# Bias loads before a memset, wide warm matmuls, early first requests and a shorter instruction stream in a gated recurrent-attention and MLP kernel

## The chip, the cores and the metric

The kernel runs on one core of a Trainium2 chip. The metric is the device time of one execution in microseconds (us), lower is better. Beside the time of each run there is one profiled execution, from which all rows below come. The engines are PE (TensorE, with its weight loads shown as PEld), DVE (VectorE), ACT (ScalarE), POOL (GpSimd) and SP (SyncE, which here only issues transfers).

## The reference

```python
g = sigmoid((x * gate_w).sum(-1))                     # x: 2048 x 512
# A: 64 segments of 32 rows, one after the other, with a memory of 8 rows
for s in range(64):
    h = concat([mem, x_s])                            # 40 rows
    q, k, v = h @ Wq, h @ Wk, h @ Wv                  # 32 heads of 128
    p = softmax(mask(q @ k.T * 128 ** -0.5))          # memory keys seen by all, the others causal
    o = (p @ v) @ Wo
    mem, out_s = o[:8], o[8:]                         # the next segment needs mem
# B: per row
y = gelu(layernorm(x) @ w1 + b1) @ w2 + b2            # inner width 1376
out = g * a + (1 - g) * y
```

All arrays are bfloat16. Part A is a chain: the memory that a segment leaves is an input of the next.

## The kernel before

The program is unrolled and the order of the instructions of each engine is written out by hand (`tc.manual_schedule()`). It has a start, a phase for part B, and 64 steps for part A.

**The start.** POOL makes the identity (`ident`, by `make_identity`), sets the last rows of `w2_sb` to zero (line 91), clears the bias tile `b1r` (line 92) and loads the bias into it by two transfers of its own queue (lines 93 and 94). SP and ACT issue the loads of `x` and of the first weights: `w1_sb` in three pieces (columns 0 to 383, then 384 to 895 by line 336, then the rest by line 337), `w2_sb` in pieces too. PE runs `NWARM = 28` matmuls of the identity on itself (line 520), 128 columns each, whose result nobody reads; then it transposes the first two normalized tiles (`prep_tr`, line 447), then the bias (line 525), and then begins part B.

**Part B.** The 16 tiles of 128 rows go in eight blocks of two. For each of 11 columns of the inner width, `a_mm` (line 468) multiplies by `w1` and ACT applies gelu with the bias; `b_mm` (line 475) follows two units later and multiplies by `w2`. Tiles in `DEF = (1, 3, 5, 7, 11, 13)` skip `b_mm` there: `spill` writes their gelu output to DRAM (`h_dr`, line 489), and the second matmul is done later, in the steps. `prep_tr` for the next block begins at unit 8 of a block whose odd tile is deferred, else at unit 6 (line 547). The weights of part A are loaded during this phase.

**The steps.** Step `s` handles segment `s`; four steps (`si` 0 to 3) make a tile. A step's PE work, in order: 64 matmuls for q and k of the 32 rows (line 127, reading `hT`), scores of half the heads (265, 269), v (146), sums of the exponentials (681, 276, 279), the other scores, the rest of v, the values (289, 294), then `wo_pass` (line 158), then `new_mem`, which transposes the new memory rows by matmuls (line 724) in three pieces, each copied by DVE into the next `hT` (line 726). The next step's q and k wait for these copies. DVE's reciprocals go through DRAM (`r_dr`, line 695) and come back broadcast (`Rb`, line 696).

Between these, work that waits for nothing fills PE's pauses. `side(T, si)` gives projections for the next tile, and in the third step of each tile `wo_left`, or for the first tile `mlp_units(8)`. The deferred matmuls come as a generator, `mlp_halves` (line 649): each deferred tile has 11 pieces, and each piece is done in two halves of four matmuls (line 656). Every step takes two halves, by two `next(mlp, None)`; `mlp_units(8)` takes 16 more in step 2. The pieces `hm` are read from DRAM by `hm_load` on SP's queue (line 634), five buffers deep: four are requested when the generator is first advanced, which is within step 0, and then one after each piece. `hm_load4` brings four more at once in step 2. After the last half of a tile, `mlp_out` (line 646) scales the sum on DVE and writes it to `c_dr`; `c_load` reads it back two tiles later.

After the last step an `If` holds a slow path for numerically bad data, which doesn't run here.

Of the kernel before, what the change touches and what calls it, by code (L numbers as in the profile page):

```python
# [27 lines left out]
def kernel(ctx, tc, A_x, A_mem0, A_Wq, A_Wk, A_Wv, A_Wo, A_seg_len, B_x, B_w1, B_b1, B_w2, B_b2, gate_w, out):  # L28
    nc = tc.nc
    P = 128  # L30
    _, S, Dm = A_x.shape
# [9 lines left out]
    FC = (F + P - 1) // P  # L41
# [20 lines left out]
    ident = pers.tile([P, P], BF16)  # L62
    g_all = pers.tile([P, NT], FP32)
    omg = pers.tile([P, NT], FP32)
    w2_sb = pers.tile([P, FC, Dm], BF16)
    c_dr = dram.tile([S, Dm], BF16, name="c_dr")
    DEF = (1, 3, 5, 7, 11, 13)
    h_dr = {T: dram.tile([FC, P, P], BF16, name=f"h_dr{T}") for T in DEF}
    r_dr = [dram.tile([P, NG], FP32, name=f"r_dr{i}") for i in range(2)]

# [17 lines left out]
    b1r = ep.tile([FC, P], BF16)  # L88
    FR = F - (FC - 1) * P
    make_identity(nc, ident[:])  # L90
    nc.gpsimd.memset(w2_sb[FR:P, FC - 1, :], 0.0)
    nc.gpsimd.memset(b1r[:], 0.0)
    nc.gpsimd.dma_start(b1r[0:FC - 1, :], B_b1[0:(FC - 1) * P].rearrange("(c p) -> c p", p=P))
    nc.gpsimd.dma_start(b1r[FC - 1:FC, 0:FR], B_b1[(FC - 1) * P:F].rearrange("(o p) -> o p", o=1))
    nc.gpsimd.memset(BO[:], 0.0)
    for g in range(4):
        nc.gpsimd.memset(BO[32 * g:32 * g + 32, 32 * g:32 * g + 32], 1.0)
# [12 lines left out]
    U = [lps.tile([P, 512], FP32, name=f"U{i}") for i in range(4)]  # L110
    X1 = lps.tile([P, 512], FP32)
# [42 lines left out]
    def wo_group(bk, U_, n):  # L154
        j, ih = HORD[n]
        for c in range(4):
            i = 4 * ih + c
            nc.tensor.matmul(bk[32 * c:32 * c + 32, :], lhsT=U_[:, j, i, :], rhs=Wo_sb[:, 4 * i + j, :],  # L158
                             start=(n == 0), stop=(n == NW - 1), tile_position=(0, 32 * c))
# [13 lines left out]
    def left_qk(T, t, hf, bk):  # L173
        for kc in range(KC):
            qk_unit(bk, gl(T), t, hf, kc)
            if kc < KC - 1:
                yield
        def ca():
            Tb = qk_cast(bk[:])
            dve_q.append(lambda: qk_tr(Tb, QL[T % 2], hf) if t == 0 else kl_tr(Tb, T, hf))  # L180
        act_q.append(ca)
        yield
# [6 lines left out]
    def left_v(T, vb, bk):  # L189
        if vb == 0:  # L190
            VLs[T] = ew.tile([P, 4, 2, Dh], BF16, tag="VL", bufs=1, name="VL")
        for kc in range(KC):
            v_unit(bk, gl(T), vb, kc)
            if kc < KC - 1:
                yield

        def ca():
            VL = VLs[T]
            nc.scalar.copy(out=VL[:, :, vb, :], in_=bk[:].rearrange("p (a e) -> p a e", a=4))

            if vb == 1:
                vp_load(T, 0)
        act_q.append(ca)
        yield
# [8 lines left out]
    def wo_left(T, bk):  # L213
        for n in range(NW):
            wo_group(bk, UL[T % 2], n)
            if n < NW - 1:
                yield

        def ca():
            wl = cw.tile([P, Dm], BF16, tag="wl", name="wl")  # L220
            nc.scalar.copy(out=wl[:], in_=bk[:])
            wls[T] = wl
        act_q.append(ca)
        yield
# [75 lines left out]
    with tc.tile_pool(name="mlpw", bufs=1) as mlpw, \  # L300
# [26 lines left out]
        w1v = B_w1.rearrange("(kc p) f -> p kc f", p=P)  # L327
        nc.sync.dma_start(w1_sb[:, :, 0:F0], w1v[:, :, 0:F0])

        NWARM = 28  # L330
        H1, H2, F1 = 3, 6, 7 * P
        for a, b in ((0, H1), (H1, H2)):
            nc.scalar.dma_start(w2_sb[:, a:b, :], B_w2[a * P:b * P, :].rearrange("(fc p) d -> p fc d", p=P))
# [109 lines left out]
        def prep_tr(blk, tt):  # L443
            y, bk = ys.pop(blk * TB + tt), (X1, X2)[tt]
            tp = bk[:].bitcast(BF16)[:, 0:Dm].rearrange("p (k t) -> p k t", k=KC)
            for kc in range(KC):
                nc.tensor.transpose(tp[:, kc, :], y[:, kc * P:(kc + 1) * P], ident[:])
            nc.vector.tensor_copy(out=yTs[blk][:, :, tt * P:(tt + 1) * P], in_=tp)
# [22 lines left out]
        def b_mm(blk, fc):  # L471
            rows = min(P, F - fc * P + 1)
            tts = [tt for tt in range(TB) if blk * TB + tt not in DEF]
            for tt in tts:
# [9 lines left out]
        def spill(blk, a, b):  # L484
            for tt in range(TB):
                T = blk * TB + tt
                if T in DEF:
                    src = hTm[blk % 2][:, :, tt * P:(tt + 1) * P]
# [27 lines left out]
        dummy = msmall.tile([P, 1], FP32, tag="dummy", name="dummy")  # L516
        nc.scalar.activation(out=dummy[:], in_=ident[:, 0:1], func=ACTF.Sqrt)

        for _ in range(NWARM):
            nc.tensor.matmul(U[3][:, 0:P], lhsT=ident[:], rhs=ident[:], start=True, stop=True, skip_group_check=True)  # L520
        b1p = W[:].bitcast(BF16)[:, 0:FC]
        prep(0)
        for tt in range(TB):
            prep_tr(0, tt)
        nc.tensor.transpose(b1p, b1r[:], ident[:FC, :FC])
        nc.vector.tensor_copy(out=b1_sb[:], in_=b1p)
        side0 = iter(())
# [2 lines left out]
        for n, (blk, fc) in enumerate(units):  # L530
# [15 lines left out]
            if blk + 1 < NBLK:  # L546
                f0 = 8 if (blk + 1) * TB - 1 in DEF else 7 if blk == 0 else 6
                if fc == 7:
# [58 lines left out]
    def chain(*gens):  # L607
        for x in gens:
            yield from x

    def side(T, si):
        gens = []
        if si == 2:
            gens = [wo_left(T - 1, X1) if T >= 1 else mlp_units(8)]
        elif T + 1 < NT:
            gens = [[left_qk(T + 1, 0, 0, X1), left_qk(T + 1, 1, 0, U[3])], [left_qk(T + 1, 0, 1, X1), left_qk(T + 1, 1, 1, U[3])], [],
                    [left_v(T + 1, 0, X1), left_v(T + 1, 1, U[3])]][si]
        return chain(*gens)
# [6 lines left out]

    work = [(T, fc) for T in DEF for fc in range(FC)]
    hms = []

    def hm_load(n):
        for _ in range(n):  # L630
            if work:
                T, fc = work.pop(0)
                hm = cw.tile([P, P], BF16, tag="hm", bufs=5, name="hm")
                nc.sync.dma_start(hm[:], h_dr[T][fc])
                hms.append((T, fc, hm, 1))
# [8 lines left out]
    def mlp_out(T):  # L644
        ct = cw.tile([P, Dm], BF16, tag="o", bufs=1, name="ct")
        nc.vector.tensor_scalar(out=ct[:], in0=W[:], scalar1=omg[:, T:T + 1], scalar2=None, op0=ALU.mult)
        nc.sync.dma_start(c_dr[T * P:(T + 1) * P, :], ct[:])

    def mlp_halves():
        hm_load(4)  # L650
        while hms:
            T, fc, hm, n = hms.pop(0)
            for h in range(2):
                cc = slice(256 * h, 256 * h + 256)
                for c in range(4):
                    nc.tensor.matmul(W[32 * c:32 * c + 32, cc], lhsT=hm[:, 32 * c:32 * c + 32], rhs=w2_sb[:, fc, cc],  # L656
                                     start=(fc == 0 and h == 0), stop=(fc == FC - 1), skip_group_check=True, tile_position=(0, 32 * c))
                if h == 1:
                    hm_load(n)
                    if fc == FC - 1:  # L660
                        mlp_out(T)
                yield

    def mlp_units(n):
        for _ in range(n):
            next(mlp, None)
            next(mlp, None)
            yield

    mlp = mlp_halves()  # L670
    XRs, Rbs = {}, {}

# [57 lines left out]
    for s in range(nseg):  # L730
        T, si = divmod(s, SPT)
        last = s == nseg - 1
        hc, hn = hT[s % 3], hT[(s + 1) % 3]
        W1, W2, W3 = WS[si]
        fill = side(T, si)
        if s + 1 < nseg:
            prep_h(s + 1)
# [134 lines left out]
    for bk, cc in halves:  # L872
        for i in range(SPT):
            nc.tensor.matmul(bk[32 * i:32 * i + 32, cc], lhsT=SelL[:, 32 * i:32 * i + 32], rhs=wl[:, cc], start=True, stop=False,
                             skip_group_check=True, tile_position=(0, 32 * i))
        for i in range(si):
            nc.tensor.matmul(bk[32 * i:32 * i + 32, cc], lhsT=SelR[:], rhs=ws[SPT * T + i][:, cc], start=False, stop=True,
                             skip_group_check=True, tile_position=(0, 32 * i))
# [4 lines left out]
    for bk, cc in halves:  # L883
        nc.tensor.matmul(bk[32 * si:32 * si + 32, cc], lhsT=SelI[:], rhs=wf[:, cc], start=False, stop=True,
                         skip_group_check=True, tile_position=(0, 32 * si))
# [125 lines left out]
```

## Time and profile before

| | before |
|---|---|
| median of 3 runs | 766.25 us (765.21 to 767.55) |
| the profiled execution's own time | 766.38 us |
| its span, first to last instruction | 764.6 us |
| mean granted TensorE clock | 0.997 |
| instructions in the trace | 44,823, of them 19,648 matmuls and as many weight loads |
| busy: PE, ACT, DVE, POOL | 97%, 70%, 52%, 36% of the span |

The profile has several views. The page gives each engine's busy time and the transfers by queue. The chain of waits follows the work that ended last back from the end: its rows have start, duration and what ran, and "issue" is time in which an engine waited for nothing that the profile shows. The view of waits sums, for each pair of waiting instruction and releaser, the total, the count and the longest. The timeline lists instructions in order of time, with the idle time before them in brackets. The view of windows gives, for stretches of time, the busy time and the count of instructions of each engine, then the granted clock, the share of the transfer engines that was busy and GB/s. The DMA view counts transfers and packets that start in a window; queue q8 of kind "instruction" carries instructions of an engine.

### The profile page before, as it was taken

What the parts mean: (1) busy time and instruction counts of PE and PEld (TensorE: products, weight loads), DVE (VectorE), ACT (ScalarE), POOL (GpSimd) and SP (SyncE); (2) the same over time, 40 slices, a digit from 0 to 9 for tenths busy, and PEclk for the clock granted to TensorE, in tenths of its full rate; (3) what the DMA queues carried; (4) which work ended last, traced back from release to release, by engine and by line L of the source; (5) the groups of instructions that cost most, each with busy time, mean ns of one, the idle gap of its engine ahead of it and who ended that gap; (6) DMA issues with size and microseconds to landing.
All of it is one profiled execution on the core that took longest, in us unless ns stands there. A gap on an engine that the chain in (4) does not pass through costs nothing.

```text
span 764.6 us, 44823 instructions
## 1 busy us (share of the span) xinstructions
PE 743.3 (97%) x19648; PEld 428.0 (56%) x19648; DVE 400.1 (52%) x1434; ACT 536.9 (70%) x1625; POOL 275.4 (36%) x517
## 2 busy tenths in 40 slices
PE   7999999999999999999999999999999999999996
PEld 5666455556555555555555655556555555555543
DVE  5877354545445454545455445545454555455444
ACT  4666676777777777777777777777777777777763
POOL 4001142443433444333443433443424443343441
PEclk9999999999999999999999999999999999999999
DMA  7999522213222212223132323222222313222211
GB/s 248 339 328 300 153 76 79 74 43 92 66 92 75 79 51 83 77 80 86 36 92 66 94 66 91 70 60 77 80 79 69 81 52 93 63 84 69 73 62 43
DMA packets 71994, 74.96 MB, mean 98 GB/s; under 512 B 39401, under 2 KB 61906, under 8 KB 70258
## 3 DMA queue, kind: packets, MB, share of 16 engines
q1 hardware_dynamic: 70354, 69.96, 29.5%
q8 instruction: 155, 2.54, 1.4%
q0 software_dynamic: 496, 1.18, 0.4%
q10 hardware_dynamic: 944, 0.92, 0.4%
q14 instruction: 45, 0.37, 0.2%
HBM read 59.13 MB, written 6.62 MB: 86 GB/s over the span
## 4 chain that ended last, share of the span: by engine, by line
PE 93%; DVE 2%; ACT 1%; DMA 1%; issue 1%; POOL 0%; DVEq 0%; POOLq 0%; ACTq 0%
PE U L127 33%; PE X L158 19%; PE X L146 16%; PE X L127 4%; PE U L289 3%; PE U L475 2%; PE SbF L468 2%; PE W L468 2%; PE W L656 2%; PE U L146 2%; PE U L265 1%; PE U L724 1%; PE SbF L265 1%; PE SbF L681 1%; DMA b1r<-in_B_b_dram 1%
## 5 line engine op out<-in xcount | busy, mean ns | idle before, releaser
L708 POOL TENSOR_TENSOR UT<-XR,Rb 128x384 bf16<-128x384 bf16 x126 | 140.3, 1137 | 300.9 <-DMA Rb<-r_dr 246.9
L132 ACT CAST Tb<-U 128x512 bf16<-128x512 f32 x288 | 168.9, 587 | 82.5 <-PE U L127 80.7
L127 PEld LDWEIGHTS <-hT 128*32 128x32 bf16 x4096 | 108.9, 96 | 100.0 <-DVE hT L726 8.7
L146 PE MATMUL X<-Wv_sb,hT 128*32 128x512 bf16 x2048 | 144.6, 378 | 0.6 <-issue 0.6
L127 PE MATMUL U<-Wq_sb,hT 128*32 128x512 bf16 x2048 | 137.0, 381 | 0.6 <-DVE hT L726 0.6
L127 PE MATMUL U<-Wk_sb,hT 128*32 128x512 bf16 x2048 | 133.4, 379 | 0.0
L158 PE MATMUL X<-Wo_sb,UT 128*32 128x512 bf16 x2016 | 122.8, 380 | 2.5 <-issue 1.0
L726 DVE CAST hT<-U 128x8 bf16<-128x8 f32 x126 | 21.0, 167 | 166.6 <-PE U L724 125.5
L786 ACT CAST V<-X 128x256 bf16<-128x256 f32 x256 | 88.7, 372 | 16.9 <-PE X L146 5.0
L136 DVE STREAM_TRANSPOSE QT<-Tb 128x256 f32<-128x256 f32 x128 | 56.6, 442 | 73.7 <-ACT Tb L132 73.5
L158 PEld LDWEIGHTS <-UT 128*32 128x32 bf16 x2080 | 59.5, 96 | 57.6 <-issue 19.4
L687 ACT CAST XR<-U 128x256 bf16<-128x256 f32 x252 | 78.4, 434 | 0.0
L715 ACT CAST w<-X 128x128 bf16<-128x128 f32 x189 | 44.7, 309 | 47.2 <-PE X L158 47.2
L136 DVE STREAM_TRANSPOSE KT<-Tb 128x256 f32<-128x256 f32 x128 | 57.0, 445 | 31.1 <-ACT Tb L132 23.2
L708 POOL TENSOR_TENSOR UL<-XR,Rb 128x128 bf16<-128x128 bf16 x126 | 60.6, 505 | 0.0
L146 PEld LDWEIGHTS <-hT 128*32 128x32 bf16 x2048 | 47.3, 94 | 21.3 <-issue 0.9
L700 POOL TENSOR_TENSOR racc<-racc,R 128x72 f32<-128x72 f32 x63 | 21.3, 338 | 101.8 <-DVE R L698 81.2
L815 ACT CAST UT<-U 128x64 bf16<-128x64 f32 x252 | 35.3, 226 | 22.5 <-PE U L294 22.5
L468 PEld LDWEIGHTS <-w_sb 128*128 128x128 bf16 (+1 forms) x352 | 34.0, 102 | 18.1 <-issue 5.5
L769 ACT ACTIVATE E<-U 128x64 bf16<-128x64 f32 (+1 forms) x128 | 35.0, 273 | 10.9 <-PE U L269 10.7
L724 PEld LDWEIGHTS <-w 128*32 128x32 bf16 x1008 | 23.7, 93 | 31.8 <-ACT w L715 25.1
L127 PE MATMUL X<-Wq_sb,GL 128*32 128x512 bf16 x496 | 39.3, 381 | 0.7 <-issue 0.7
(169 smaller groups left out, 1236.7 us busy)
## 6 DMA issues: line engine op xcount, KB each, us to landing
Rb<-r_dr SPq DMA_DIRECT2D x63, 512.0 KB, 3.8
Wv_sb<-in_A_Wv_dram SPq DMA_DIRECT2D x4, 1024.0 KB, 6.4
Wq_sb<-in_A_Wq_dram SPq DMA_DIRECT2D x4, 1024.0 KB, 7.4
Wk_sb<-in_A_Wk_dram SPq DMA_DIRECT2D x4, 1024.0 KB, 8.8
Wo_sb<-in_A_Wo_dram SPq DMA_DIRECT2D x4, 1024.0 KB, 11.8
VP<-VL SPq DMA_DIRECT2D x64, 64.0 KB, 3.2
c<-c_dr SPq DMA_DIRECT2D x16, 128.0 KB, 3.2
hm<-h_dr SPq DMA_DIRECT2D x62, 32.0 KB, 3.3
```

What stands on the lines that cost most here:

```text
L127: nc.tensor.matmul(bk[32 * j:32 * j + 32, :], lhsT=G[:, kc, :], rhs=W5[t][:, kc, h0:h1, j, :], start=(kc == 0), stop=(kc == KC - 1), tile_ ...
L132: nc.scalar.copy(out=Tb[:], in_=bk.rearrange("p (a b e) -> p a e b", a=8, b=2))
L136: nc.vector.transpose(out=dst[:, 8 * hf:8 * hf + 8, c0:c0 + 32, :].rearrange("p a r b -> p a (r b)").bitcast(FP32), in_=Tb[:].rearrange("p ...
L146: nc.tensor.matmul(bk[32 * j:32 * j + 32, :], lhsT=G[:, kc, :], rhs=Wv5[:, kc, 4 * vb:4 * vb + 4, j, :], start=(kc == 0), stop=(kc == KC - ...
L158: nc.tensor.matmul(bk[32 * c:32 * c + 32, :], lhsT=U_[:, j, i, :], rhs=Wo_sb[:, 4 * i + j, :], start=(n == 0), stop=(n == NW - 1), tile_po ...
L468: nc.tensor.matmul(hp[:rows, 0:TB * P], lhsT=w1_sb[:, kc, fc * P:fc * P + rows], rhs=yTs[blk][:, kc, :], start=(kc == 0), stop=(kc == KC - 1))
L687: nc.scalar.copy(out=XR[:, j], in_=U[j][:, 0:NG * 40].rearrange("p (i q) -> p i q", q=40)[:, :, 0:32])
L708: nc.gpsimd.tensor_tensor(out=out[:, :, 4 * h:4 * h + 4, o:o + b - a], in0=XR[:, :, 4 * h:4 * h + 4, a:b], in1=Rb[:, h, :, :, a:b], op=ALU ...
L715: nc.scalar.copy(out=w[:, a:b], in_=bk[:, a:b])
L769: nc.scalar.activation(out=E[:, 4 * i2:4 * i2 + 4, c], in_=Sb[i2][:, :, c], func=ACTF.Exp, scale=scale)
L786: nc.scalar.copy(out=V[:, i0:i0 + 2, :].rearrange("p i e -> p (i e)"), in_=(X1, X2)[vb][:, 256 * h:256 * h + 256])
L815: nc.scalar.copy(out=UT[s % 2][:, j, :, 0:M], in_=U[j][:, 0:NG * 40].rearrange("p (i q) -> p i q", q=40)[:, :, 32:40])
```

## The change

Six edits:

1. The memset of `w2_sb`'s last rows goes behind the two bias loads on POOL.
2. The 28 warm matmuls of 128 columns become 13 of 512 columns (the identity read four times over), and two more of these stand between the first transposes and that of the bias.
3. `DEF` has tile 9 in place of tile 7.
4. `mlp_units(8)` becomes `mlp_units(7)`.
5. The first four requests of `hm` are made ahead of the steps, right after part B, and no more at the generator's first advance.
6. What follows from 2 and 4: 13 pairs of weight load and matmul and 8 matmuls with their weight loads, 42 instructions, are gone from PE's order ahead of steps 3 to 58; one instruction that only waits has come in within step 0. From step 59 on the 16 instructions of edit 4 have been made up. SP's queue has its first four `hm` requests ahead of the `VP` load and the `xT` load of step 0, where before they were behind them.

```diff
--- before.py
+++ after.py
@@ -64,7 +64,7 @@
     omg = pers.tile([P, NT], FP32)
     w2_sb = pers.tile([P, FC, Dm], BF16)
     c_dr = dram.tile([S, Dm], BF16, name="c_dr")
-    DEF = (1, 3, 5, 7, 11, 13)
+    DEF = (1, 3, 5, 9, 11, 13)
     h_dr = {T: dram.tile([FC, P, P], BF16, name=f"h_dr{T}") for T in DEF}
     r_dr = [dram.tile([P, NG], FP32, name=f"r_dr{i}") for i in range(2)]
 
@@ -88,10 +88,10 @@
     b1r = ep.tile([FC, P], BF16)
     FR = F - (FC - 1) * P
     make_identity(nc, ident[:])
-    nc.gpsimd.memset(w2_sb[FR:P, FC - 1, :], 0.0)
     nc.gpsimd.memset(b1r[:], 0.0)
     nc.gpsimd.dma_start(b1r[0:FC - 1, :], B_b1[0:(FC - 1) * P].rearrange("(c p) -> c p", p=P))
     nc.gpsimd.dma_start(b1r[FC - 1:FC, 0:FR], B_b1[(FC - 1) * P:F].rearrange("(o p) -> o p", o=1))
+    nc.gpsimd.memset(w2_sb[FR:P, FC - 1, :], 0.0)
     nc.gpsimd.memset(BO[:], 0.0)
     for g in range(4):
         nc.gpsimd.memset(BO[32 * g:32 * g + 32, 32 * g:32 * g + 32], 1.0)
@@ -327,7 +327,7 @@
         w1v = B_w1.rearrange("(kc p) f -> p kc f", p=P)
         nc.sync.dma_start(w1_sb[:, :, 0:F0], w1v[:, :, 0:F0])
 
-        NWARM = 28
+        NWARM = 13
         H1, H2, F1 = 3, 6, 7 * P
         for a, b in ((0, H1), (H1, H2)):
             nc.scalar.dma_start(w2_sb[:, a:b, :], B_w2[a * P:b * P, :].rearrange("(fc p) d -> p fc d", p=P))
@@ -516,12 +516,16 @@
         dummy = msmall.tile([P, 1], FP32, tag="dummy", name="dummy")
         nc.scalar.activation(out=dummy[:], in_=ident[:, 0:1], func=ACTF.Sqrt)
 
-        for _ in range(NWARM):
-            nc.tensor.matmul(U[3][:, 0:P], lhsT=ident[:], rhs=ident[:], start=True, stop=True, skip_group_check=True)
+        def warm(n):
+            for _ in range(n):
+                nc.tensor.matmul(U[3][:].rearrange("p (a b) -> p a b", a=4), lhsT=ident[:], rhs=ident[:].unsqueeze(1).to_broadcast([P, 4, P]), start=True, stop=True, skip_group_check=True)
+
+        warm(NWARM)
         b1p = W[:].bitcast(BF16)[:, 0:FC]
         prep(0)
         for tt in range(TB):
             prep_tr(0, tt)
+        warm(2)
         nc.tensor.transpose(b1p, b1r[:], ident[:FC, :FC])
         nc.vector.tensor_copy(out=b1_sb[:], in_=b1p)
         side0 = iter(())
@@ -611,7 +615,7 @@
     def side(T, si):
         gens = []
         if si == 2:
-            gens = [wo_left(T - 1, X1) if T >= 1 else mlp_units(8)]
+            gens = [wo_left(T - 1, X1) if T >= 1 else mlp_units(7)]
         elif T + 1 < NT:
             gens = [[left_qk(T + 1, 0, 0, X1), left_qk(T + 1, 1, 0, U[3])], [left_qk(T + 1, 0, 1, X1), left_qk(T + 1, 1, 1, U[3])], [],
                     [left_v(T + 1, 0, X1), left_v(T + 1, 1, U[3])]][si]
@@ -647,7 +651,6 @@
         nc.sync.dma_start(c_dr[T * P:(T + 1) * P, :], ct[:])
 
     def mlp_halves():
-        hm_load(4)
         while hms:
             T, fc, hm, n = hms.pop(0)
             for h in range(2):
@@ -667,6 +670,7 @@
             next(mlp, None)
             yield
 
+    hm_load(4)
     mlp = mlp_halves()
     XRs, Rbs = {}, {}
 
```

## The prediction

> **What bounds the kernel now.** I read the page first, for which engine carries the time.
>
> ```profile
> PE 743.3 (97%) x19648; PEld 428.0 (56%) x19648; DVE 400.1 (52%) x1434; ACT 536.9 (70%) x1625; POOL 275.4 (36%) x517
> ...
> q8 instruction: 155, 2.54, 1.4%
> ```
>
> TensorE (PE) is busy 97% of the span; every other engine has room. So only two things shorten the kernel: less PE work, or fewer moments in which PE stands or is slowed. The change removes almost no work (13 of 19,648 matmuls), so I looked for the moments. The view of PE's waits names one in the first step (and one at the start, in part 4); the chain of waits, in order of time, gives the beginning of each step (its 64 matmuls of line 127), and with that a quiet measure to hold the others against.
>
> ```profile
> PE W L656 <- DMA hm<-h_dr: 1.2, 1, 1.2
> ```
>
> ```profile
> 109.55 3.55 PE U L127 x64
> ...
> 131.51 3.55 PE U L127 x64
> ...
> 465.60 3.55 PE U L127 x64
> ...
> 486.31 3.55 PE U L127 x64
> ...
> 506.78 3.55 PE U L127 x64
> ...
> 673.51 3.55 PE U L127 x64
> ```
>
> These rows begin steps 2, 4, 36, 38, 40 and 56. Steps 36 to 39, one whole tile, took 506.78 - 465.60 = 41.18 us, with no long wait in them. Steps 4 to 55 are 13 tiles: at that pace 535.3 us, but they took 673.51 - 131.51 = 542.0. So **6.7 us** are lost there. Steps 2 and 3 took 21.96 us, where 38 and 39 took 20.47: another **1.5 us**.
>
> Where do the 6.7 us go? I looked at one slow step (17) in the chain of waits, and at the DMA view of the tenth of a microsecond before the stop:
>
> ```profile
> 273.69 0.33 issue
> 274.02 0.61 PE X L127 x6
> ```
>
> ```profile
> q8 instruction: 1, 0.02, 72.0%
> ```
>
> PE stops inside a run of equal matmuls, where no semaphore is waited for ("issue"). The second row is the DMA view of 271.6 to 271.7 us: one instruction packet starts there, and 72% of 16 engines for 0.1 us is 1.15 us, so it ends at about 272.8, 1.2 us before PE goes on. The page counts 155 such packets; 39,296 PE instructions (two times 19,648) over 155 are 254 each. PE's instructions arrive in blocks of about 256, and PE here has used one up before the next is in. If so, stops lie at whole blocks from each other. Between four of them, by the view of windows:
>
> ```profile
> 180.34:211.69 31.35, 31.27 (x894) 19.85 (x895) 16.29 (x58) 22.44 (x71) 11.85 (x22) 1.00 0.22 66
> 211.69:274.01 62.32, 62.00 (x1789) 35.59 (x1789) 32.29 (x114) 45.88 (x144) 24.60 (x44) 1.00 0.27 80
> 274.01:305.61 31.60, 31.26 (x894) 17.20 (x894) 15.11 (x55) 22.86 (x73) 12.96 (x25) 1.00 0.26 72
> ```
>
> PE and weight loads together are 1,789, 3,578 and 1,788; with one wait instruction a step that the view doesn't count, 1,792, 3,584 and 1,791: 7, 14 and 7 blocks, to one instruction. Numbered by the program's order, these stops, and the others of the slow steps, fall on the same place of a block (instruction 194 or 195 of 256).
>
> **Part 1: 41 instructions less, and what they do to the loop.** Fifteen warm matmuls instead of 28 take 26 PE instructions out (weight load and matmul each), one unit less in step 2 takes 16 more, and the new order has one wait instruction more: steps 3 to 58 begin 41 earlier in the stream. So each block boundary falls 41 instructions later within its step. A step has 593 instructions (609 every fourth), so boundaries drift slowly; in steps 4 to 56 they now sit in bands at 17-49, 98-133, 192-221, 273-305, 354-389, 448-477 and 529-561. The changed bands: 58-90, 139-174, 233-262, 314-346, 395-430, 489-518, 570-602. What matters is how fast PE runs through the 256 instructions behind a boundary. Stretches of 256 (the first row a stalled one, the next four from the undisturbed step 18, starting at offsets 208, 139, 233 and 262; edge instructions count twice):
>
> ```profile
> 270.66:274.01 3.35, 3.04 (x134) 1.90 (x127) 2.32 (x9) 2.60 (x13) 1.25 (x4) 1.00 0.02 5
> 281.99:284.66 2.67, 2.67 (x132) 1.75 (x129) 1.88 (x9) 2.06 (x10) 1.11 (x4) 1.00 0.02 6
> 280.82:283.86 3.04, 3.04 (x136) 1.93 (x132) 2.05 (x6) 2.46 (x8) 2.12 (x4) 1.00 0.00 0
> 282.08:285.30 3.22, 3.22 (x144) 2.02 (x140) 1.94 (x8) 2.63 (x13) 1.67 (x5) 1.00 0.04 6
> 282.20:285.97 3.77, 3.77 (x146) 2.27 (x141) 1.94 (x8) 3.18 (x14) 1.66 (x5) 1.00 0.04 5
> ```
>
> The band 192-221 sits before the shortest stretch of the whole step: short matmuls of the scores, the row sums and the values, 2.67 us. When the block comes late, the same stretch takes 3.35, and the other stops show 2.95 to 3.46. In the changed kernel the shortest stretch behind any boundary is 3.04, the next 3.22 to 3.77, all others 3.8 or more. A delivery that takes 2.95 to 3.46 us mostly fits. The lower bound of what stays is nothing. The upper: 18 boundaries in band 139-174, half of them late by 0.25 (3.3 less 3.04), 2.2 us. I take 1.2, since a request there follows long matmuls, of which more are queued ahead in time. Loop: 6.7 - 1.2 = **-5.5** (bounds -6.7 to -4.5 by this reading; 0 by the rival below).
>
> [...]
>
> **Part 2: steps 2 and 3.** Line 615 now runs 7 units in step 2, not 8. With 8, the first deferred tile ends inside step 2's tail, and its output runs on VectorE between the casts that the next step waits for:
>
> ```profile
> 120.73 0.75 DVE L646 TENSOR_SCALAR ct<-W,omg 128x512 bf16<-128x512 f32 x1
> ...
> 121.40 0.16 DVE L726 CAST hT<-SbF 128x16 bf16<-128x16 f32 x1
> ...
> 121.62 0.62 PE L127 MATMUL U<-Wq_sb,hT 128*32 128x512 bf16 x8 [0.41 <-DVE hT L726]
> ```
>
> The cast at 121.40 stood behind the 0.75 us of line 646, and PE idled 0.41 (0.56 against the usual order). With 7, the tile ends at the second piece of step 3, where later tiles end too. The other 0.9 of the 1.5 us is a block stop in step 2; its boundary moves from offset 243 to 268, before a stretch of over 3.77 us. So **-1.4** (bounds -0.5 to -1.5). The moved unit's 8 matmuls take about 0.2 out of step 2 and land in step 58, which waits for other engines: **-0.1** (bounds -0.2 to 0).
>
> **Part 3: first pieces ahead of the steps.** SyncE's queue, in order of time, and the landing in the chain:
>
> ```profile
> 89.04 0.54 SPq L187 DMA_DIRECT2D VP<-VL  x1
> 89.62 1.27 SPq L101 DMA_TRANSPOSE xT<-in_A_x_dram  x1
> 91.39 3.26 SPq L634 DMA_DIRECT2D hm<-h_dr  x5
> 95.55 0.32 SPq L695 DMA_DIRECT2D r_dr<-R  x1
> ```
>
> ```profile
> 91.39 2.63 DMA hm<-h_dr
> ```
>
> The first piece is asked for at 91.39 and lands at 94.02; PE, ready at 92.87, waits 1.2 us. Moved ahead of the loads for steps 1 and 8, the four requests start where those stood, at 89.04, and the first lands near 91.7. PE is then not held. The two loads that slip behind them go out some 2.6 us later; the first is read a step afterwards, the second in step 3. The write of R, next in the queue, went out at 95.55, 0.9 after the fifth request; that stays, since as many requests stand ahead of it. I take **-1.0** of 1.2 (bounds -1.2 to 0), because the boundary of step 0 moves to offset 184, whose stretch lies between the 2.67 and the 3.04 above, with transfers beside it.
>
> **Part 4: the start.** The chip's queues at the start, PE's rows, and two windows with the granted clock (last column but two):
>
> ```profile
> 1.01 0.52 POOL L91 MEMSET w_sb<- 32x512 bf16 x1
> ...
> 1.97 3.17 PE L520 MATMUL U<-ident 128*128 128x128 bf16 x28 [1.97 <-POOL ident masks.py:199]
> ...
> 6.46 0.72 PE L447 MATMUL X<-ident,y 128*128 128x128 bf16 x8 [1.32 <-DVE y L440]
> ...
> 9.22 0.16 PE L525 MATMUL W<-ident,b1r 11*128 11x11 bf16 x1 [2.04 <-DMA b1r<-in_B_b_dram]
> ...
> 12.28 0.69 PE L468 MATMUL W<-yT,w_sb 128*128 128x256 bf16 x4
> ```
>
> ```profile
> 5.62:9.03 3.41, 0.72 (x8) 0.45 (x8) 1.66 (x5) 1.62 (x3) 3.40 (x20) 1.00 1.10 357
> 9.03:12.45 3.42, 3.23 (x15) 2.19 (x16) 2.72 (x12) 1.30 (x3) 0.56 (x2) 0.50 1.05 347
> ```
>
> ```profile
> w_sb<-in_B_w_dram SPq DMA_DIRECT2D x1, 512.0 KB, 8.9
> ```
>
> The 0.52 us memset of line 91 stood ahead of the identity and the bias loads. Behind them, the identity is ready some 0.3 earlier (the bias tile's own small memset now comes first) and the bias some 0.5: PE's transposition at 9.22 comes to about 8.7. The clock was halved from 9.03 to 12.45, after a window with 0.72 us of PE work. Thirteen wide warm matmuls, each four times 3.17/28, are 5.9 us at that pace, from 1.65 to at most 7.5; they then hold the transposes at 6.46 by up to 1 us, which the bias, there at 8.7, about covers. PE works longer in the window, so the clock may hold. Either way the fourth block of weights, the last row (asked for at 2.69), lands at 11.6, and the matmuls that need it began at 12.28. So at most 0.7 is to be had; I take **-0.6** (bounds -0.7 to 0).
>
> [...]
>
> **Part 5: tile 9 deferred instead of 7.** The same 11 matmuls move from block 4 to block 3; the spill's two DMAs move with them. I cost this at **0** (bounds -0.5 to +0.5, the size of one wait of PE for an activation between blocks).
>
> Sum: -5.5 - 1.4 - 0.1 - 1.0 - 0.6 = -8.6. The profiled execution took 766.4 us (span 764.6 and 1.8 around it), as the median of the runs, 766.25. So **757.8**.
>
> **Rivals.** *Stops return elsewhere.* Block delivery isn't tied to these stretches, and as many stops turn up in other steps: the loop gains nothing, the rest 3.1: 763.3. For it: of the 18 passes through the fast stretch only some stopped, so chance is at work. Against: all sit on the one fastest stretch. *Slower: delivery is slower than the new stretches.* If a block takes not 2.95-3.46 but 3.6 us at the new places, because requests there meet the loads of the step's middle, 18 boundaries lose 0.56 at 3.04 and as many some 0.2 at 3.22-3.77: 13.3 us, for 6.7 saved; with the other 3.1 saved, 769.9. It decides from about 3.5 (18 times 0.46, and 9 times 0.15 in the early half of the next band: 9.7). Against it: 3.46 is the longest seen, with transfers beside. *The front costs.* Part 3 gains nothing and part 5 loses 0.5: 759.3.
>
> **How the numbers follow.** Forecast 0.70, stops elsewhere 0.17, slower 0.06, front costs 0.07. The range reaches from 755.0 (no stop left, all bounds at their best: 9.9 off, and 1 for the tail and the start's chance) up to 763.0, which takes in the front's case and half of the first rival. A measurement tells 0.3%, 2.3 us, from no change: faster means under 763.95. The forecast, the front's case and two thirds of the first rival are that: 0.89. Same: 0.06. Slower: 0.05.
>
> **What would show it.** Right: from the start of step 4 to that of step 56 about 536.5 us; hardly an issue stop of over 0.3 us before line 158; no wait for hm in step 0; line 646 out of step 2's tail; the fourth block of weights used at 11.6 to 11.8. Wrong: the 52 steps at 540 or more (rival one), or steps of 10.5 and more in long rows (rival two).

## The result: a third of the forecast

The changed kernel takes 765.03 us (median of 22 runs, 763.52 to 767.89), the kernel before 767.55 beside it (22 runs, 762.93 to 770.30): a ratio of 0.9972, interval 0.9959 to 0.9985. That is 2.5 us less, where 8.6 less and a time of 757.8 (755.0 to 763.0) were forecast. The forecast's start, one profiled execution at 766.38 and three runs around it, was itself low: the median of all 22 runs is 1.2 us higher. Of the 8.6 us, 5.5 were to come from the loop, and there nothing was saved.

The page of the changed kernel, PE's busy time and the instruction packets:

```profile
PE 744.7 (97%) x19624; PEld 423.4 (55%) x19635; DVE 401.0 (52%) x1434; ACT 537.1 (70%) x1625; POOL 275.1 (36%) x517
...
q8 instruction: 155, 2.54, 1.4%
```

PE is as busy as before (743.3 us) and gets as many packets (155). The beginnings of steps 2, 4 and 56 in the chain of waits (start, duration, what ran):

```profile
108.02 3.55 PE U L127 x64
...
128.53 3.55 PE U L127 x64
...
674.37 3.55 PE U L127 x64
```

Steps 2 and 3 took 20.51 us (21.96 before), as forecast. Steps 4 to 55 took 545.84, where 542.0 had been and 536.5 was forecast. PE's waits (total, count, longest) name the stops, first in the kernel before, then in the changed one:

```profile
PE X L158 <- issue: 1.0, 2, 0.6
```

```profile
PE U L289 <- issue: 4.1, 10, 0.6
...
PE W L659 <- DMA hm<-h_dr: 1.2, 1, 1.2
...
PE W L468 <- DMA w_sb<-in_B_w_dram: 0.6, 1, 0.6
```

The first row of the changed kernel is new: stops for nothing visible, now inside the values (line 289), where before the view put them in line 158 and a few others. The next is the wait for `hm` of step 0 (line 656 before), exactly as long as it was. One of the new stops, in step 36, by the chain, and the DMA view of 469.5 to 469.6 us:

```profile
464.58 3.55 PE U L127 x64
...
471.52 0.59 issue
```

```profile
q8 instruction: 1, 0.02, 62.6%
```

The same picture as before: a packet of 62.6% of 16 engines for 0.1 us, that is 1.00 us, ends at about 470.5, and PE goes on at 472.11, 1.6 us later (1.2 in step 17 of the kernel before). What moved is the place. The start of the program, PE's rows, one window (last columns: granted clock, DMA share, GB/s) and the chain's piece that sets its end:

```profile
1.47 5.73 PE L521 MATMUL U<-ident 128*128 128x512 bf16 x13 [1.47 <-POOL ident masks.py:199]
...
8.11 0.18 PE L529 MATMUL W<-ident,b1r 11*128 11x11 bf16 x1
8.37 0.60 PE L468 MATMUL SbF<-yT,w_sb 128*128 128x256 bf16 x4
...
10.99 0.61 PE L468 MATMUL W<-yT,w_sb 128*128 128x256 bf16 x4 [0.65 <-DMA w_sb<-in_B_w_dram]
```

```profile
9.03:12.45 3.42, 2.65 (x21) 1.70 (x19) 2.94 (x16) 2.00 (x5) 0.44 (x2) 1.00 1.06 350
```

```profile
2.69 8.25 DMA w_sb<-in_B_w_dram
```

The bias is transposed at 8.11 (9.22 before), the granted clock behind it is 1.00 (0.50 before), and the fourth block is used at 10.99, when its weights land (12.28 before). The first step begins at 85.94 for 87.31.

### The profile page after: what moved, and what is told of

Same layout as the page of the kernel before. It is cut to its first block, busy times and chain, and to the rows that moved or that the text cites. A ratio compares the mean times of both kernels' runs of the same rounds, so it can differ in the third digit from the quotient of the medians.

```text
span 765.4 us, 44786 instructions
## 1 busy us (share of the span) xinstructions
PE 744.7 (97%) x19624; PEld 423.4 (55%) x19635; DVE 401.0 (52%) x1434; ACT 537.1 (70%) x1625; POOL 275.1 (36%) x517
## 4 chain that ended last, share of the span: by engine, by line
PE 93%; DVE 3%; DMA 2%; issue 1%; ACT 1%; SPq 0%; DVEq 0%; ACTq 0%
PE U L127 33%; PE X L158 19%; PE X L146 16%; PE X L127 4%; PE U L289 3%; PE W L468 2%; PE U L475 2%; PE W L659 2%; PE U L146 2%; PE SbF L468 2%; PE U L265 1%; DMA w_sb<-in_B_w_dram 1%; PE U L728 1%; PE SbF L265 1%; PE SbF L685 1%
## 5 line engine op out<-in xcount | busy, mean ns | idle before, releaser
L158 PEld LDWEIGHTS <-UT 128*32 128x32 bf16 x2080 | 56.5, 96 | 60.7 <-issue 17.8
L127 PE MATMUL U<-Wk_sb,GL 128*32 128x512 bf16 x496 | 39.9, 377 | 0.0
## 6 DMA issues: line engine op xcount, KB each, us to landing
Wo_sb<-in_A_Wo_dram SPq DMA_DIRECT2D x4, 1024.0 KB, 11.1
```

The costliest lines, as they stand in the source:

```text
L127: nc.tensor.matmul(bk[32 * j:32 * j + 32, :], lhsT=G[:, kc, :], rhs=W5[t][:, kc, h0:h1, j, :], start=(kc == 0), stop=(kc == KC - 1), tile_ ...
```

## The experiments

Two tables collect what the runs e1 to e12 showed; the two that remain, e13 and e14, follow below. "Plus" and "minus" count PE instructions ahead of the steps. "Stops" is worked out from each trace: at every block boundary of steps 4 to 55, the time by which the 14 instructions around it took longer than in an undisturbed pass of the kernel before, summed where it is over 0.08 us. "Loop" is the time of these 52 steps in the one profiled execution.

| boundaries as in | kernel | loop, us | stops, us |
|---|---|---|---|
| before | before | 542.0 | 6.6 |
| | e1, changed, plus 42 | 544.6 | 6.9 |
| | e6, e9, e10 (start edits on before) | 543.9, 545.0, 545.1 | 7.6, 8.0, 9.2 |
| changed | changed, two executions | 545.8, 544.4 | 10.4, 8.6 |
| | e2, before, minus 42 | 544.1 | 7.9 |
| | e5, e7, e11 (changed, one edit or two) | 543.9, 543.6, 545.0 | 8.5, 8.2, 9.4 |
| others | e4, plus 36 | 543.2 | 6.5 |
| | e3, plus 12 | 548.9 | 12.8 |
| | e12, plus 60 | 543.4 | 7.2 |

Each loop less its stops is 535.4 to 537.7 us, beside the 535.3 at which the forecast's undisturbed pace comes out: the stops at block boundaries are most of what the loops lose, in every one of these kernels.

The medians of e1 to e12 stand beside the kernel before's, run together with them (769.1 to 769.8); only the ratios are to be compared with each other.

| kernel | median, us | ratio to before | interval |
|---|---|---|---|
| e1 / e2 | 766.6 / 768.5 | 0.9973 / 0.9993 | 0.9956-0.9990 / 0.9979-1.0008 |
| e3 / e4 | 768.8 / 768.1 | 0.9997 / 0.9988 | 0.9981-1.0014 / 0.9973-1.0002 |
| e5 / e6 | 766.1 / 767.2 | 0.9965 / 0.9978 | 0.9950-0.9980 / 0.9964-0.9992 |
| e7 / e8 | 765.3 / 766.1 | 0.9949 / 0.9962 | 0.9931-0.9968 / 0.9942-0.9982 |
| e9 / e10 | 768.6 / 768.2 | 0.9981 / 0.9979 | 0.9962-0.9999 / 0.9958-0.9999 |
| e11 / e12 | 765.4 / 769.2 | 0.9942 / 0.9997 | 0.9920-0.9966 / 0.9980-1.0013 |

**The place of the boundaries.** Cutting a wide warm matmul into four narrow ones keeps its columns and adds 6 PE instructions, so the boundaries can be moved alone.

```diff
-        warm(NWARM)
+        warm(NWARM - 7)          # e1; 2 in e3, 6 in e4, 10 in e12
+        for _ in range(28):      # 8 in e3, 24 in e4, 40 in e12
+            nc.tensor.matmul(U[3][:, 0:P], lhsT=ident[:], rhs=ident[:], ...)
```

> The changed kernel with 7 of its 13 wide warm matmuls cut into four narrow ones each: the same columns, 42 PE instructions more, so every block boundary of steps 3 to 58 sits where it sat in the kernel before. Theory 'place' (what the loop loses is set by where the boundaries fall; the new places are bad ones because a request between offsets 133 and 174 doesn't go out before the scores' wait at about 4.1 us of the step is over): the 52 steps from 4 to 55 return from 545.8 to 542 us (540.5 to 543.5), the time is about 3.7 us under the changed kernel, 761.3. Theory 'order' (the loop lost by tile 9, the early hm requests or the moved unit, and the places are nothing): 545.8 and 765, as the changed kernel.

Measured: loop 544.6, time as the changed kernel's. 'Place' asked for 542 and missed; 'order' asked for 545.8 and missed by 1.2.

> The kernel before with its 28 narrow warm matmuls as 7 wide ones: the same columns, 42 PE instructions less, nothing else changed. 'Place': boundaries sit as in the changed kernel; the 52 steps go from 542.0 to 545.5 (544 to 547.5), the time rises by 2.5 to 5 over the kernel before, with stops at offsets 395 to 430 and 489 to 518 of nearly every pass. 'Order': 542 and no change. My forecast on record had the places right and would want 536.5.

Here the 28 narrow warm matmuls are 7 wide ones. Loop 544.1, the time 0.5 us under the kernel before, within its interval. The loop is at the low edge of what 'place' gave (544 to 547.5), but 'place' had the time 2.5 to 5 slower: wrong. The stops did move to offsets 406 to 431 and 490 to 515 (4.6 and 2.2 us of them).

> The changed kernel with 2 wide warm matmuls cut into four each, 12 PE instructions more: boundaries at 127-162 and 221-250 of a step in place of 139-174 and 233-262. 'Place', by a replay of the observed delays: the worst of the places tried, 1 to 2 us over the changed kernel (52 steps at 547, time 766.5). 'Order': 545.8 and 765.

The worst place, as 'place' had it: 12.8 us of stops, loop 548.9, and by the ratio almost all of the change's gain is lost. This profiled execution (770.76) was 2.0 us above the median of its kernel, so the size may be too high.

> The changed kernel with 6 wide warm matmuls cut into four each, 36 PE instructions more: boundaries at 103-138 and 197-226. 'Place', by the same replay: about the best place, like plus 42 or up to 1 us better (52 steps at 541.5, time 761). 'Order': 545.8 and 765.

Few stops (6.5 us), loop 543.2; the median does not show it as better (ratio 0.9988).

After these four neither theory stood: the place decides where PE stops, and at plus 12 how much, but before's place and the changed one came out nearly alike. The profiled execution of the kernel before, 542.0, began to look like luck.

**The same kernel again.**

> The changed kernel as it is, for a second profiled execution and a ratio on this chip. The profiled executions so far stand at different heights against their own medians (the kernel before 1.2 below, the changed kernel 2.1 above). Theory 'chance': much of the 3.8 us by which the loop (steps 4 to 55) got longer is that: 543.7 us in an average execution, 543 to 545 here. Theory 'place': the new places of the boundaries cost it in each execution: 545.5 or more. The ratio to the kernel before 0.996 to 0.998.

```profile
128.76 3.55 PE U L127 x64
...
673.19 3.55 PE U L127 x64
```

The chain's steps 4 and 56 are 544.43 us apart, 1.4 less than in the first execution of the same kernel. With all runs in hand: five executions at before's place 542.0 to 545.1, mean 544.1; six at the changed place 543.6 to 545.8, mean 544.5. The difference is 0.4, its standard error 0.65. 'Chance' holds: the loop neither gained nor lost anything that can be told (the eight kernels beside the two are alike in the loop's PE work, but not in all else), and the profile of before, from which the forecast took its 542.0, is the shortest of five.

**Is any place free?**

> The changed kernel with 10 wide warm matmuls cut into four each, 60 PE instructions more: boundaries at 79-114, 173-202, 254-286 of a step. So far the stops in steps 4 to 55 summed to 6.5 to 6.9 us at plus 36, plus 42 and in the kernel before, 7.8 to 10.4 at the changed kernel's place, 12.8 at plus 12. Theory 'zone': requests from about offset 133 to 260 are late, and neighbouring bands are some 84 apart, so at least one band lies in that zone wherever the boundaries are put: 5 to 8 us of stops here too, the loop 542.5 to 545. Theory 'free place' (my forecast's): a place whose stretches are long enough has hardly a stop: under 2 us, the loop under 539.

Loop 543.4, stops 7.2, 6.3 of them at offsets 429 to 454: 'zone'. No place that was tried had under 6.5 us of stops. This execution (766.01) was 3.1 us below its kernel's median of 769.15, so an average one may have more.

**Why the zone is late.** In the traces of before, e1 and e4, whose band lies across offset 131, 44 of the 45 packets of boundaries up to 131 start 2.2 to 3.6 us into the step, the six behind it at 2.8 to 4.7; in the changed kernel's band of 149 to 174 not one of 17 starts before 4.13. The scores' wait stands at offset 127, four instructions ahead of that divide; why the two don't coincide isn't known. What is waited for, a transposition on DVE, ends at 3.1 us of the step (median), and all 17 packets of the changed kernel's band start at least 1.0 us behind that. In e3, with its band at 137 to 162, three of 17 (at 137 to 141) start at 3.3 to 3.8, the others at 4.1 or later. The next two runs moved the wait.

```diff
+        for kc in range(KC):
+            v_unit(X1, hc, 0, kc)
         scores(s, 0)
         nc.scalar.activation(out=E[:, 0:4, :], in_=Sb[0], func=ACTF.Exp, scale=scale)
-        for kc in range(KC):
-            v_unit(X1, hc, 0, kc)
```

> The changed kernel with the first 16 matmuls of v (32 instructions) ahead of the first scores: the boundaries stay, the scores' wait moves from offset 127 to 159 of a step. Theory 'held by the wait': packets of boundaries at 149 to 158 start before 3.6 us of the step (in the changed kernel none did before 4.1), those at 160 to 174 still not before 4.1. Rival 'time of the step': all still at 4.1 or later. The time itself gets worse by some 3 to 6% either way, since the sums now stand right behind the scores and wait for the exponentials; it is not what is asked.

> The same with 12 PE instructions more ahead of the steps: boundaries at 137 to 162, so that 14 of 17 stand ahead of the moved wait; to be held against e3, where they stood behind it. 'Held by the wait': these 14 packets start before 3.6 us of the step, for about 4.2 in e3; the few stops that remain at offsets 393 to 418 belong to boundaries at 160 to 162. 'Time of the step': about 4.2 again. The time 3 to 6% worse, as above.

The same boundary of step 30 (offset 148), in e3 by the chain and the DMA view of 409.3 to 409.4 us, then in e14 by the chain and the view of 414.9 to 415.0:

```profile
405.41 3.55 PE U L127 x64
```

```profile
q8 instruction: 1, 0.02, 58.3%
```

```profile
411.78 3.55 PE U L127 x64
```

```profile
q8 instruction: 1, 0.02, 66.6%
```

From the step's row to the packet it is 3.9 us in e3 and 3.1 in e14. Counted from the step's first matmul, 0.15 earlier, over the 14 boundaries at 137 to 156 of both kernels the median start goes from 4.25 to 3.4 us, 11 of the 14 now before 3.6, and the stops at 393 to 418 fall from 4.0 to 0.2 us. The arrival of PE itself doesn't explain it: its weight loads reach these boundaries at 3.5 to 3.7 us in e3 and at 3.5 to 4.1 in e14, so the packets went out earlier although PE came later. In e14 'held by the wait' is borne out, and 'time of the step' falls.

In e13 neither theory's expectation holds. The packets at 149 to 174 start at 3.4 to 5.9 (4.1 to 5.2 in the changed kernel). Of the five at 149 to 157, which should have come before 3.6, two did; of those at 160 to 174, which should have stayed at 4.1 or later, five came before 3.9. The expected cut between 159 and 160 is not there. The wait that was moved is for the transposition that ends at 3.1, and PE's weight loads reach 160 at 4.2 only, so it may hold hardly anything at its new place; what then delays the late half is not shown. The kernels themselves are 2.5% and 2.8% slower than before, as the sums now wait for the exponentials (weight loads of the sums waited 37.2 us for them in each, 14.3 in the changed kernel); those idle times give the block some time too, so it is the packet's start in e14, and not the stops alone, that carries this.

**The first pieces.** e5 undoes edit 5. e7 gives the first piece a buffer of its own in place of one that lies over part B's memory:

```diff
+    hm0 = pers.tile([P, P], BF16)
...
-                hm = cw.tile([P, P], BF16, tag="hm", bufs=5, name="hm")
+                hm = hmb[hmn[0] % 5]      # hmb: hm0 and four tiles of cw
+                hmn[0] += 1
```

> The changed kernel with the first four hm requests made at the generator's first advance again. My forecast on record: one microsecond slower than the changed kernel. Theory 'held behind': the early request did nothing, since the wait for hm was 1.2 in both kernels and the piece landed 1.2 us after the end of the same instruction packet in both: step 0 stays at 11.7, the wait at 1.0 to 1.3, the time at that of the changed kernel (within 0.5).

Measured: wait 1.2 us, median 766.12 for 766.10 in e8. The edit is worth nothing.

> The changed kernel, with the first hm piece in a buffer of its own (5 buffers taken in turn as before, but the first of them not over memory that part B has used, so that its request need not wait for the last c_dr write, which landed at 88.95). Theory 'buffer': the request goes out near 87.7 and the piece lands by 91, PE's wait of 1.2 us goes, step 0 takes 10.5 to 10.7 for 11.8, the time falls by about 1.1 under the changed kernel. Theory 'something else is late next' (the instruction block, a cast): the wait goes but step 0 gets back less than 0.4. Theory 'held behind the instruction packet': the landing stays at 92.7 whatever the request.

SP's request and PE's first use in e7; then one step later DVE, POOL and PE; then the same DVE instruction in e8:

```profile
87.61 3.84 SPq L641 DMA_DIRECT2D hm<-h_dr  x4
```

```profile
91.26 0.29 PE L662 MATMUL W<-w_sb,hm 128*32 128x256 bf16 x4
...
103.66 0.28 PE L289 MATMUL U<-E,V 32*128 32x40 bf16 x16 [0.61 <-DVE E L784]
```

```profile
102.47 1.13 DVE L784 TENSOR_TENSOR E<-E,RS 128x64 bf16<-128x64 bf16 x1
```

```profile
102.42 2.17 POOL L715 TENSOR_TENSOR UT<-XR,Rb 128x384 bf16<-128x384 bf16 x2 [8.43 <-DMA Rb<-r_dr]
```

```profile
103.62 0.28 DVE L781 TENSOR_TENSOR E<-E,RS 128x64 bf16<-128x64 bf16 x1
```

The wait is gone and step 0 takes 10.36 for 11.6 to 11.8: the request goes out at 87.61 as 'buffer' said, and a landing that stays "whatever the request", the form that 'held behind the instruction packet' had, falls. But where the request and the packet overlap, the piece still lands behind the packet. The trace records sixteen landings of one such transfer. In the changed kernel fifteen lie at 90.56 to 90.91 and the last at 92.69, 1.1 us after the end of an instruction packet (90.25 to 91.56). In e5 the request goes out 0.8 later, at 89.97, and the last still lands at 92.64, 1.3 after the packet's end. In all 14 executions of this case in which the two overlap, the last landing follows the packet's end by 1.0 to 1.3 us. In e7 all sixteen lie at 89.16 to 89.47, before the packet starts at 90.07; in e11 it is the same. So the buffer of its own helps because the request gets ahead of the packet.

Step 1, however, takes 11.02 for 10.16: its DVE multiplication now starts 0.05 after a pass of POOL and takes 1.13 for 0.28, and PE waits 0.61 for it. Of 1.3 us 0.4 to 0.5 is left, and the ratio (0.9949 for 0.9962) doesn't resolve it.

**The start.** e6 has edits 1 and 2 on the kernel before with as many PE instructions as before (9 wide, 17 narrow and 2 wide matmuls), e9 edit 1 alone, e10 the warm work of e6 alone.

> The kernel before with the start edits alone (bias loads ahead of the memset, the warm work as 9 wide and 17 narrow matmuls and two wide ones ahead of the bias's transposition: as many PE instructions as before, so the block boundaries don't move). Theory 'the start gives all of the front': the first step begins 1.3 to 1.4 us earlier than before's 87.31, near 85.95, the fourth block of weights is used near 11.0, steps 0 to 3 stay at 44.0, the time is 1.3 under the kernel before. By my forecast on record 0.6, with the fourth block at 11.6. If tile 9 for 7 gave part of it, the first step begins later than 86.3.

Measured: first step at 85.95, fourth block at 10.97, steps 0 to 3 44.0, ratio 0.9978: the start edits give all of the front, tile 9 nothing.

> The kernel before with one edit: the memset of w2_sb's last rows behind the two bias loads. Theory 'clock': what the start gains comes from the wide warm matmuls, which keep PE at full speed: here four matmuls of line 468 take 1.03 as before, the fourth weight block is used near 11.6, the first step begins at 86.6 to 87.3. Theory 'bias': the earlier transposition of the bias gives it: used near 11.0, first step near 86.0. My forecast on record gave this edit 0.5 at the transposition.

> The kernel before with the warm work as 9 wide and 17 narrow matmuls and two wide ones ahead of the bias's transposition, the memset where it was; as many PE instructions as before. 'Clock': line 468 takes 0.60 per four at once, the fourth weight block is used when it lands, near 10.9 to 11.6, the first step begins near 86.0 to 86.5. 'Bias': transposition at 9.2, first step at 87 or later.

PE's rows in e9, then in e10:

```profile
8.09 0.17 PE L525 MATMUL W<-ident,b1r 11*128 11x11 bf16 x1 [0.48 <-DMA b1r<-in_B_b_dram]
8.18 1.03 PE L468 MATMUL SbF<-yT,w_sb 128*128 128x256 bf16 x4
...
10.94 0.61 PE L468 MATMUL W<-yT,w_sb 128*128 128x256 bf16 x4
```

```profile
8.71 0.16 PE L530 MATMUL W<-ident,b1r 11*128 11x11 bf16 x1
8.89 0.60 PE L467 MATMUL SbF<-yT,w_sb 128*128 128x256 bf16 x4
...
11.12 0.61 PE L467 MATMUL W<-yT,w_sb 128*128 128x256 bf16 x4 [0.26 <-DMA w_sb<-in_B_w_dram]
```

Each alone did it in these executions: the first step begins at 85.91 and 86.07. With the bias early, PE runs at the slow pace (1.03) but has begun so early that it is there at 10.94; with wide matmuls it begins later at full pace and waits for the weights at 11.12. Both theories had named one cause where either was enough here, since the weights' landing (near 10.9 and 11.1) capped both. Chance had a part in each. In e9 PE's matmuls were back at full pace after 10.5 us, where in the kernel before they were slow until 12.5. In e2, where the bias also came early (8.49), they were slow until 13.5, and the first step began at 87.62: an early bias with the slow pace is not always enough. And in e10 the bias came at 8.71 for 9.22, without an edit that would bring it forward.

**A further step.** e11 is e7 with the 512 KB load split, columns 384 to 511 first.

> The kernel of e7 (own buffer for the first hm piece) and the 512 KB load of w1's columns 384 to 895 in two: columns 384 to 511 first, then the rest. In the changed kernel PE waits 0.5 to 1.5 us for that load at 10.9. Theory 'size': the smaller first load lands before 10.3, the wait goes, the next block waits a little at most: first step at 85.2 to 85.5 for 85.9, 0.5 under e7, 1.5 under the changed kernel. Theory 'shared': the load's landing is set by all that is on the way (350 GB/s moved), the small one lands as late: no gain.

```profile
10.45 0.60 PE L469 MATMUL W<-yT,w_sb 128*128 128x256 bf16 x4
```

The fourth block waits for nothing, although the bias came late in this execution (8.53); the first step begins at 85.52, 0.36 earlier than in e7. 'Size' holds: the smaller load lands at 9.95, and the first step begins at the upper edge of its range. The ratio, 0.9942, is the lowest of all, but its interval doesn't tell it from e7's.

## Why the prediction was wrong

**Part 1, the loop: -5.5 forecast, about 0 measured (+0.4, standard error 0.65).** This is the step that failed: "the shortest stretch behind any boundary is 3.04", so "a delivery that takes 2.95 to 3.46 us mostly fits". Blocks, places and bands were right; the stops stood at the offsets that the bands say. But a delivery has no fixed length behind its boundary: when its packet starts depends on the place, as the runs show. Behind offset 131 it seems to wait for the scores (a median of 4.25 us of the step in e3, 3.4 in e14 with that wait moved; e13 leaves this open): a boundary at 149 to 174 gets its packet at 4.1 to 5.2 us of the step (median 4.5), not much before one at 192 to 217 got it (4.2 to 5.9, median 4.9), while PE needs it earlier: by the kernel before's median pass offset 405 is reached at 6.6 us and 448 at 6.9. The rest, "a request there follows long matmuls, of which more are queued ahead in time", was sized at 1.2 and is some 5 in that band alone (4.6 to 6.4), with 1.9 to 3.2 in the next. A longer lead behind long matmuls was the author's estimate: in the kernel before the packets of boundaries at 108 to 131 do start 0.1 to 0.8 us ahead of PE's weight loads there, but in the changed kernel those at 149 to 174 start 0.5 to 1.6 us behind them. The late zone, offsets 133 to about 260, is wider than the distance of neighbouring bands (some 84), so one band or two are always in it; 0.7 to 2.4 us of the stops lie outside it. The rival "stops return elsewhere" (763.3, 3.1 us saved) is what happened.

Part of the miss was the reading: the 542.0 of one execution was taken for the kernel's loop, where the mean at its place is 544.1. Executions of one kernel differ by 1.4 us in it (changed kernel), those at one place by 3.1.

**Part 2: -1.4 forecast, -1.45 in the profile.** Both halves are shown apart. Step 3 takes 10.79 and 10.80 with eight units (before, e2) and 10.22 and 10.22 with seven (changed, e1). Step 2 takes 11.17 and 11.32 at before's place (before, e1), 10.28 to 10.83 at the changed one (changed, e2, e5, e8): its stop is worth 0.3 to 1.0, so some of the 1.45 was chance. The moved unit: steps 56 to 62 took 72.21 and then 72.13, the -0.1.

**Part 3: -1.0 forecast, 0 measured (e5).** Of the step "the four requests start where those stood, at 89.04, and the first lands near 91.7" the second half failed:

```profile
89.15 2.80 SPq L638 DMA_DIRECT2D hm<-h_dr  x4
```

```profile
89.15 3.54 DMA hm<-h_dr
```

The request went out at 89.15 but took 3.54 for 2.63: the last of its sixteen landings followed the instruction packet that ended at 91.56, as it does in e5 with the later request. The forecast took 2.63 for the transfer's own length, though there, too, the last landing (94.03) came 1.2 after a packet's end (92.85). And as all else had moved 1.4 earlier, the request should have gone out at 87.7, as it does in e7; its buffer held it until it met the packet (SP's queue waited there for a `c_dr` write of part B, 1.1 us in the two waits of this kind).

**Part 4: -0.6 forecast, -1.37 measured.** Right in mechanism (the cap is the weights' landing), mis-sized in the cap: 11.6 was this load's landing in the execution of before; in the runs it lands at 10.7 to 11.6, and mostly near 10.9 with the bias ahead. That the slow pace, which in the kernel before lasted until 12.5, would go with it was left open in the forecast; in the changed kernel it was gone (3.33 us of PE work from 5.62 to 9.03 for 0.72, and a granted clock of 1.00 behind it for 0.50).

**Part 5: 0 forecast, 0 measured** (85.95 in e6, 85.94 and 85.77 in the changed kernel).

Two sums of the forecast are off, and nothing hangs on them: 18 times 0.56 and 18 times 0.2 are 13.7, not 13.3, and all bounds at their best add up to 10.8, not 9.9.

## What to carry to other kernels

The stops that recurred at a fixed distance in the instruction stream were not cured by shifting the stream (6.5 to 12.8 us of them at every place tried). Of such stops, ask when the packet for the next block starts and which wait stands ahead of the boundary (4.25 us of the step in e3, 3.4 in e14 with a wait moved), not only how long the stretch behind it lasts, and how many places of a period are late. Before a forecast of some microseconds rests on one profiled execution, look how far executions of the same kernel lie apart. Of a request that is moved up in a queue, ask what its buffer was last used for (the first `hm` went out at 89.15 into part B's memory, at 87.61 into a buffer of its own) and whether it overlaps an instruction packet (the last landing then came 1.0 to 1.3 us after the packet's end, whether the request had gone out at 89.15 or at 89.97).

## What the runs showed of the hardware

The packet of PE's next block started before PE's weight loads reached the boundary in step 18 of the kernel before (2.31 us of the step for 2.89). With the scores' wait moved behind 14 boundaries, their packets started at a median of 3.4 us of the step in e14 for 4.25 in e3; e13 did not show the same. What sends the request out was not shown.

The first `hm` transfer, where it overlapped an instruction packet, had the last of its sixteen landings 1.0 to 1.3 us after the packet's end, in 14 of 14 executions.

DVE's 128x64 multiplication of `E` by `RS` took 0.22 to 0.23 us whenever no POOL operation ran at its start. Where a POOL tensor operation with more than 0.26 us left to run was under way, which was so 66 times in the first fourteen profiles (before, changed, e1 to e12), it was never under 0.30. It ended 0.08 after POOL's operation in e7 (103.60 for 103.53, hence 1.13) and in e8 (103.90 for 103.82, hence 0.28). The same multiplication with `SbF`, which PE's matmuls write, in place of `RS` took under 0.30 in all 251 such cases. In e1 11 of 63 multiplications with `RS` took 0.48 to 0.96 us (median 0.23), in e8 none did: a second source of chance in the loop, beside the blocks.
